# Window attention and experts on one core: the heads of five groups turned on VectorE, shorter weight prefetch, another place for the row scatter

## The chip, the core and the metric

The kernel runs on one core of one Trainium2 chip. The metric is the device time of one execution in microseconds. A core has five engines that run their own instruction streams in order: TensorE (PE in the profile, with its weight loads shown apart as PEld), VectorE (DVE), ScalarE (ACT), GpSimd (POOL) and SyncE (SP, which here only starts transfers). They wait for each other through semaphores.

## What is computed

Two things in a row. First, attention over a window of 64 positions for 8 batches, 8 heads, 576 positions and 64 values a head:

```
scores = (q @ k.T) / 8;  masked where not 0 <= pos_i - pos_j < 64
attn   = exp(scores - max) / (sum + 1e-9)
out    = attn @ v
```

Then each of the 4608 rows (512 values, all heads side by side) goes to one of 8 experts, the one with the largest logit:

```
logits = x @ w_gate + modality_bias[modality_id]
e      = argmax(logits);  gate = softmax(logits)[e]
out    = gate * (relu(x @ w1[e]) @ w2[e])        # w1: 512x1024, w2: 1024x512
```

All in 32-bit floats. The expert matmuls are done with numbers split in two parts (`Whi`, `Wlo` for weights, `xh`, `xl` and `hh`, `hl` for rows), three products for one.

## The kernel before

**Attention** goes in 36 steps `s` of 128 positions (a pair of blocks of 64). Two steps make a group `G`, 18 in all; a group has four blocks. For a step the scores of its blocks need `q` and `k` with the head's values on the partitions, so each group's `q` and `k` are turned first, one step or two ahead: step `s` turns parts of group `s // 2 + 1`, `k` in even steps, `q` in odd ones, four heads in `part(0)` and four in `part(1)`. A part is turned in one of two ways. By TensorE: four 128x128 transposes into a PSUM tile `tp` (`heads_t`, line 594, recorded under the helper's line 470), then a copy out of it on VectorE or ScalarE (`heads_out`, line 605). Or by VectorE alone: one transpose of 32x32 blocks from SBUF to SBUF (`turn_heads`, line 568), which needs the heads loaded in another layout, in pieces of 32 values, by eight requests for four heads (line 590) in place of two (line 584). Before the change seven late groups, those from group 8 on whose four blocks lie in one batch, have four heads in each way.

**Experts** begin while attention is still running: from step 12 on (`FIRST`), each step has up to four gaps, and at each gap `gap(it, True)` records one piece of expert work: six or twelve matmuls of a slot of 256 rows (`first`, line 304, and `second`, line 326). What a piece leaves to other engines is put in `later` and recorded by the next `run_later()`. The end of a slot's first or second 128 rows is `finish` (line 332): VectorE scales the result into a tile `y` (line 334), GpSimd scatters it to the output (line 337).

**Rows** reach the experts through a scratch in HBM: `route1` to `route3` find expert and place, and two scatters by GpSimd (line 809) write a group's rows. From group 4 on they are held back (`held`) and issued by `release()`, which in a step with gaps stands ahead of the first gap. It also records what is left of the routing on VectorE, and the conversion of the indices (line 821).

**Weights** of the first two experts come in 32 raw pieces. Each `weights(s)` call takes one older piece on VectorE (`split_lo`, line 119), one on ScalarE (`split_hi`, line 114), and loads new ones until two are in flight. The raw pieces and the results of `finish` use the same four buffers, `y`. A buffer is given to whoever asks next after its last reader is recorded.

The order on all engines is the order in which this code records instructions (the schedule is manual). `at` is a table of loads by step: values, then `k` or `q` of a later group, all requests on SyncE's queue, recorded at one place in the middle of a step. Group `G >= 8` loads `k` in step `2G-3` and `q` in step `2G-2` into two buffers `qk`; each is turned one step later. The framework gives each request started from SyncE or ScalarE one of eight semaphores in turn, and a request waits until the one that had the semaphore before has landed.

Of the kernel before, what the change touches and what calls it, by code (L numbers as in the profile page):

```python
# [20 lines left out]
W64 = 64  # L21
# [5 lines left out]
def tile_window_attn_moe(  # L27
# [12 lines left out]
    nc = tc.nc  # L40
    B, H, S, D = q.shape
# [4 lines left out]
    HP = H // 2  # L46
    R32 = 32
# [199 lines left out]
    def run_later():  # L247
        while later:
            later.pop(0)()
# [243 lines left out]
    def by_group(x):  # L493
        return x.rearrange("p (a h j) i -> p a h j i", a=2, h=HP)
# [8 lines left out]
    qk = {}  # L503
# [3 lines left out]

    PARTS = ((K0, K1), (Q0, Q1))
    AHEAD = range(1, 8)
    QUARTERS = 8  # L510
    WARM = 8, 3

    n_tp = [0]
# [36 lines left out]
        else:  # L550
            qk[G, nm] = work.tile([P, 2, H, D], F32, name="qk", bufs=2)

    def quartered(G):

        return G >= QUARTERS and GBLK * G // BPB == (GBLK * G + GBLK - 1) // BPB

    def plain(t, nh):

        return t.rearrange("p t h d -> p (t h d)")[:, 0:2 * nh * D].rearrange("p (t h d) -> p t h d", t=2, d=D)

    def by_heads(t):

        return t.rearrange("p t h d -> p (t h d)")[:, H * D:].rearrange("p (h u d) -> p h u d", h=HP // 2, d=R32)

    def turn_heads(G, nm, i):

        dst = by_group(qT if nm == "q" else kT)[:, G % 2, 2 * i:2 * i + 2]
        nc.vector.transpose(
            out=dst.rearrange("p h j i -> p (h j i)"),
            in_=by_heads(qk[G, nm]).rearrange("p h u d -> p (h u d)"))  # L570

    def load_qk(G, nm, blocks=range(GBLK), dma=nc.sync):

        t = qk[G, nm]
        x = q if nm == "q" else k
        i = blocks[0]
        while i <= blocks[-1]:
            b, g = divmod(GBLK * G + i, BPB)
            n = min(BPB - g, blocks[-1] + 1 - i)
            nh = HP if quartered(G) else H  # L580
            src = x[b, 0:nh, g * W64:(g + n) * W64].rearrange("h (p t) d -> p t h d", t=2)
            p0 = i * W64 // 2
            for par in range(2):
                dma.dma_start(out=plain(t, nh)[p0:p0 + n * W64 // 2, par], in_=src[:, par])
            u = slice(i * W64 // R32, (i + n) * W64 // R32)
            for h in range(nh, H):
                for c in range(2):
                    rows = slice((h % 2 * 2 + c) * R32, (h % 2 * 2 + c + 1) * R32)
                    src = x[b, h, g * W64:(g + n) * W64, c * R32:(c + 1) * R32]
                    dma.dma_start(out=by_heads(t)[rows, (h - nh) // 2, u, :],  # L590
                                  in_=src.rearrange("(u p) d -> p u d", p=R32))
            i += n

    def heads_t(G, nm, i, tp):


        src = plain(qk[G, nm], HP if quartered(G) else H).rearrange("p t (h a) d -> p t h (a d)", a=2)
        for h in range(2):
            for t in range(2):
                n = 2 * h + t  # L600
                turn(tp[:, n * P:(n + 1) * P], src[:, t, 2 * i + h])
# [135 lines left out]
    def release():  # L737

        if held:
            tick(len(routing))  # L740
            held.pop(0)()
# [142 lines left out]
    def when(step, f, *args):  # L884
        at.setdefault(max(step, -1), []).append((f, args))
# [9 lines left out]
    for G in range(1, NG):  # L895
        ahead = 1 if G in AHEAD else 0
        for nm, step in (("k", 2 * G - 3 - ahead), ("q", 2 * G - 2 - ahead)):
            when(step, new_qk, G, nm)
            when(step, load_qk, G, nm)

    pieces = []
    raws = []
# [144 lines left out]
    def weights(s):  # L1047

        if halves:
            split_lo(*halves.pop(0))  # L1050
        if len(raws) == 2 or raws and not pieces:
            split_hi(*raws[0])
            halves.append(raws.pop(0))
        while pieces and len(raws) < 2:
            x, c = pieces.pop(0)
            raw = epool.tile([P, WCH], F32, name="y", bufs=4)
            raws.append((load_piece(raw, evs[x], c), x, c))

    for s in range(NPR + 4):
# [7 lines left out]
        heads = PARTS[j] if G < NG else ()  # L1067
        R = (s - 5) // GB if s >= 5 and j == 1 else -1

        def part(i):  # L1070
            if not heads:
                return
            if i == 1 and quartered(G):
                turn_heads(G, *heads[1])
                return
            tp = turn_bank(s)
            heads_t(G, *heads[i], tp)
            heads_out(tp, G, *heads[i], nc.scalar.copy if heads[i] == K1 else nc.vector.tensor_copy)
# [59 lines left out]
            cnt = ranks()  # L1138
            exps(s, (5, 6, 7))
        else:  # L1140
            release()
            gap(it, True)
            run_later()
            tick(2)
            if s < NPR:
                exps(s, (2, 3, 4))
            if s < FIRST + 4 or s % 2:
                weights(s)
            for f, args in at.pop(s, ()):
                f(*args)  # L1150
            gap(it, True)
            cnt = ranks()
            if s < NPR + 2:
# [1 line left out]
            part(0)  # L1155
            run_later()
            tick(n_tick)
            if s < NPR:
                exps(s, (5, 6, 7))
        if n_gap > 2:  # L1160
# [3 lines left out]
        part(1)  # L1164
        run_later()
        tick(n_tick)
        if s == WEIGHTS:
            load_weights()
        if s >= WEIGHTS:
            weights(s)  # L1170
        if n_gap > 3:
            gap(it, True)
        run_later()
# [278 lines left out]
```

## Time and profile before

| | |
|---|---|
| median of 3 runs | 629.34 us (627.99 to 630.23) |
| the profiled execution | 624.07 us, its span 622.3 us |
| granted TensorE clock, mean over the span | 0.989 |
| PE busy | 600.2 us, 96% of the span |
| DVE, ACT, POOL busy | 389.3, 293.7, 140.9 us |

Steps are told apart in the trace by their scores matmuls (line 640), 32 in each step: those of step 16 start at 117.23 us, of step 17 at 127.91, of step 25 at 216.22, of the last, step 35, at 320.84. In the timeline a row has the start, the duration, the engine (PEld and SPq, ACTq are weight loads and transfer starts), the line, the operation, output<-input, the shapes, how many were merged, and in brackets the idle time of the engine ahead of it with what ended it.

### The profile page before, as it was taken

Reading aid. Unit: us, or ns where it says so; the run is one execution under the profiler, and the core shown is the slowest. Engines: PE = TensorE matmul, PEld = TensorE weight load, DVE = VectorE, ACT = ScalarE, POOL = GpSimd, SP = SyncE. Lnnn points to the kernel's source line nnn. Section 1 sums busy time; section 2 is a strip of 40 time slices with the busy share of each in tenths; the row PEclk is TensorE's granted clock in tenths of the full one; section 3 lists DMA queues with packets and bytes.
Section 4 is the critical chain, followed back from the end, with each engine's and each line's share of the span. In section 5 each row is a group of like instructions: output and inputs, shape, how many; then the busy total and the mean of one; then the engine's idle time right before and its main releaser. Section 6 shows DMA issues by size and latency. Waiting matters only on the chain.

```text
span 622.3 us, 17338 instructions
## 1 busy us (share of the span) xinstructions
PE 600.2 (96%) x6309; PEld 537.6 (86%) x6309; DVE 389.3 (63%) x1493; ACT 293.7 (47%) x926; POOL 140.9 (23%) x315
## 2 busy tenths in 40 slices
PE   7999889979999989999999999999999999999996
PEld 5888778868889878988898899899999999989986
DVE  3899988857867776767656365323224734776621
ACT  3899885753756556555553111111112513554411
POOL 6333322132142212320423131011001111102202
PEclk7999999999999999999999999999999999999999
DMA  9998957656757735554513034622243534678300
GB/s 167 219 242 213 223 159 181 158 152 152 171 152 183 197 84 137 154 111 102 148 53 105 35 101 151 188 71 69 44 159 101 171 135 136 190 252 241 114 17 22
DMA packets 175111, 88.08 MB, mean 142 GB/s; under 512 B 138746, under 2 KB 157744, under 8 KB 174896
## 3 DMA queue, kind: packets, MB, share of 16 engines
q1 hardware_dynamic: 166400, 67.46, 44.6%
q0 software_dynamic: 5888, 18.93, 8.1%
q8 instruction: 50, 0.82, 0.5%
q10 hardware_dynamic: 2736, 0.58, 0.5%
q14 instruction: 37, 0.30, 0.2%
HBM read 67.49 MB, written 23.91 MB: 147 GB/s over the span
## 4 chain that ended last, share of the span: by engine, by line
PE 70%; DVE 5%; DMA 5%; SPq 3%; issue 2%; ACT 2%; POOL 1%; POOLq 0%; DVEq 0%; ACTq 0%
PE y L326 27%; PE em L304 19%; PE sp L304 10%; PE tp L470 6%; PE av L696 2%; PE sp L640 2%; DMA out_dram<-y,id 2%; SPq L590 2%; DMA xs_scratch<-xa,idx 1%; PE tp L725 1%; DVE xt L266 1%; PE y L377 1%; DMA xt<-xs_scratch 1%; DVE xl L196 1%; POOL xs_scratch L809 1%
## 5 line engine op out<-in xcount | busy, mean ns | idle before, releaser
L326 PE MATMUL y<-Whi,hh 128*128 128x512 f32 x288 | 116.3, 404 | 0.0
L666 ACT ACTIVATE ss<-ss,mn 128x128 f32<-128x128 f32 x288 | 112.2, 397 | 6.6 <-DVE mn L654 6.6
L326 PE MATMUL y<-Wlo,hh 128*128 128x512 f32 x288 | 113.2, 393 | 0.0
L326 PE MATMUL y<-Whi,hl 128*128 128x512 f32 x288 | 112.9, 392 | 0.0
L313 DVE SCALAR_TENSOR_TENSOR hl<-em,hh 128x512 fp32r<-128x512 f32 x50 | 34.4, 689 | 79.5 <-ACT hh L312 79.1
L337 POOL DMA_INDIRECT out_dram<-y,id x36 | 39.7, 1104 | 191.0 <-DVE y L334 160.8
L304 PE MATMUL em<-xh,Whi 128*128 128x256 f32 x400 | 81.7, 285 | 0.0
L304 PE MATMUL em<-xl,Whi 128*128 128x256 f32 x400 | 79.2, 279 | 0.0
L304 PE MATMUL em<-xh,Wlo 128*128 128x256 f32 x400 | 79.1, 279 | 0.0
L312 ACT ACTIVATE hh<-em 128x512 fp32r<-128x512 f32 x50 | 29.9, 599 | 100.5 <-PE em L304 95.5
L675 ACT COPY pT<-tp 128x512 f32<-128x512 f32 x57 | 31.5, 589 | 83.3 <-PE tp L470 83.0
L809 POOL DMA_INDIRECT xs_scratch<-xa,idx x36 | 36.6, 1017 | 128.9 <-DVE e_n_p L154 58.9
L326 PEld LDWEIGHTS y<-Whi,hl 128*128 128x128 f32 x288 | 54.3, 189 | 12.2
L654 DVE CUSTOM_DVE_ANT_0 ss<-sp,masks 128x128 f32<-128x128 f32 x288 | 63.4, 285 | 2.3 <-PE sp L640 2.3
L304 PEld LDWEIGHTS em<-xh,Whi 128*128 128x128 f32 x400 | 62.8, 188 | 2.3
L326 PEld LDWEIGHTS y<-Whi,hh 128*128 128x128 f32 x288 | 54.7, 190 | 8.9
L326 PEld LDWEIGHTS y<-Wlo,hh 128*128 128x128 f32 x288 | 54.5, 189 | 8.5
L304 PEld LDWEIGHTS em<-xh,Wlo 128*128 128x128 f32 x400 | 60.9, 188 | 0.0
L304 PEld LDWEIGHTS em<-xl,Whi 128*128 128x128 f32 x400 | 60.8, 188 | 0.0
L666 ACT ACTIVATION_READ_ACCUMULATOR ss<-ss,mn 128x1 f32 x288 | 55.9, 194 | 0.0
L312 ACT ACTIVATE hh<-sp 128x512 fp32r<-128x512 f32 x22 | 13.1, 597 | 76.1 <-PE sp L304 76.1
L696 PEld LDWEIGHTS av<-ve,pT 128*64 128x64 f32 x576 | 36.3, 138 | 12.6 <-issue 8.1
(242 smaller groups left out, 1201.7 us busy)
## 6 DMA issues: line engine op xcount, KB each, us to landing
xt<-xs_scratch SPq DMA_DIRECT2D x72, 128.0 KB, 2.9
vo<-in_v_dram SPq DMA_DIRECT2D x32, 256.0 KB, 3.3
y<-in_moe_w_dram SPq DMA_DIRECT2D x32, 256.0 KB, 2.8
vo<-in_moe_w_dram SPq DMA_DIRECT2D x24, 256.0 KB, 3.6
ss<-in_moe_w_dram SPq DMA_DIRECT2D x24, 256.0 KB, 4.2
xs_scratch<-xs_scratch SPq DMA_DIRECT2D x8, 514.0 KB, 5.8
pT<-in_moe_w_dram SPq DMA_DIRECT2D x16, 256.0 KB, 4.5
qk<-in_k_dram SPq DMA_DIRECT2D x22, 128.0 KB, 3.9
```

Of the source, the lines that this page charges most:

```text
L304: nc.tensor.matmul(out=hb[:, i * TP:(i + 1) * TP], lhsT=w[buf][:, c0:c0 + P], rhs=x[:, c * TP:(c + 1) * TP], start=(n == 0), stop=(n == le ...
L312: nc.scalar.activation(out=hh, in_=hb, func=AF.Relu),
L313: nc.vector.scalar_tensor_tensor(out=hl, in0=hb, scalar=0.0, in1=hh.bitcast(F32), op0=ALU.max, op1=ALU.subtract)))
L326: nc.tensor.matmul(out=sl["y", t], lhsT=h[:, i * TP + t * P:i * TP + (t + 1) * P], rhs=w[buf][:, c0:c0 + DM], start=(k == 0 and n == 0), s ...
L337: ins = nc.gpsimd.indirect_dma_start(out=out, out_offset=bass.IndirectOffsetOnAxis(ap=sl["id"][:, t:t + 1], axis=0), in_=y, in_offset=None ...
L470: nc.tensor.transpose(out=out_, in_=in_, identity=ident[p0:p0 + n, p0:p0 + n])
L590: dma.dma_start(out=by_heads(t)[rows, (h - nh) // 2, u, :], in_=src.rearrange("(u p) d -> p u d", p=R32))
L654: nc.vector.tensor_tensor_reduce(out=ss[a][:, hp, :], in0=sp[a][:, hp * P:(hp + 1) * P], in1=mask, scale=-1.0 / 8.0, scalar=3.0e38, op0=AL ...
L666: nc.scalar.activation(out=ss[a][:, hp, :], in_=ss[a][:, hp, :], func=AF.Exp, bias=mn[:, h:h + 1], scale=-1.0, accum_out=sm[:, h:h + 1])
L675: nc.scalar.copy(out=pT, in_=pp)
L696: nc.tensor.matmul(out=by_block(av)[c * W64:(c + 1) * W64, a, :, hp, :], lhsT=pT[:, i:i + W64], rhs=(vo if c else ve)[p][:, 2 * hp + a, :] ...
L809: ins = nc.gpsimd.indirect_dma_start(out=xs, out_offset=bass.IndirectOffsetOnAxis(ap=idx[:, j:j + 1], axis=0), in_=xg[j], in_offset=None)
```

## The change

Four edits.

1. Groups 10, 12, 14, 16 and 17 (`WHOLE`) have all eight heads turned by VectorE. Groups 8 and 9 (`HALF`) stay as they were; the others are turned by TensorE as before. `n_plain(G)` is the number of heads that TensorE turns.
2. In the five groups the loads of all heads are pieces of 32 values: 16 requests for a tensor in place of 10, and every fourth (odd head, second half) is started by ScalarE. From group 8 on a tensor's loads are several entries of the table, for two heads each (the first four heads of a `HALF` group are one entry), and `loads(n)` records them at four places of a step instead of one.
3. From step 16 on, one raw weight piece is in flight instead of two.
4. `release()` stands behind the first gap and `run_later()` instead of ahead of them.

```
-    QUARTERS = 8
+    HALF = 8, 9
+    WHOLE = 10, 12, 14, 16, 17
...
+    def n_plain(G):
+
+        return 0 if G in WHOLE else HP if G in HALF else H
...
     def load_qk(...)
-            for h in range(nh, H):
+            for h in hs if hs[0] >= nh else ():
                 for c in range(2):
...
-                    dma.dma_start(out=by_heads(t)[rows, (h - nh) // 2, u, :],
-                                  in_=src.rearrange("(u p) d -> p u d", p=R32))
+                    other = nh == 0 and h % 2 and c
+                    (nc.scalar if other else dma).dma_start(
+                        out=by_heads(t, nh)[rows, (h - nh) // 2, u, :],
+                        in_=src.rearrange("(u p) d -> p u d", p=R32))
...
-            when(step, load_qk, G, nm)
+            for h in (0, *range(max(n_plain(G), 2), H, 2)) if n_plain(G) < H else (0,):
+                when(step, load_qk, G, nm, range(GBLK), nc.sync, range(h, h + 2))
...
     def weights(s):
-        if len(raws) == 2 or raws and not pieces:
+        n = 2 if s < FIRST + 4 else 1
+        if len(raws) >= n or raws and not pieces:
...
-        while pieces and len(raws) < 2:
+        while pieces and len(raws) < n:
...
         def part(i):
-            if i == 1 and quartered(G):
-                turn_heads(G, *heads[1])
+            if 2 * 2 * i >= n_plain(G):
+                turn_heads(G, *heads[i])
                 return
...
         else:
-            release()
             gap(it, True)
             run_later()
+            release()
             tick(2)
...
-            for f, args in at.pop(s, ()):
-                f(*args)
+            loads(3)
...
             run_later()
             tick(n_tick)
+            loads(1)
...
         part(1)
         run_later()
         tick(n_tick)
+        if s > FIRST:
+            loads(1)
...
         if s >= WEIGHTS:
             weights(s)
+        if s > FIRST:
+            loads(9)
```

How the order of instructions moves, at three places. First GpSimd at step 16, which is the first of six steps (16, 20, 24, 28, 32, 36) in which a held pair of row scatters meets the result of a slot (`xs_scratch<-xa` is the scatter of rows, `out_dram<-y` that of a result). Before:

```order
L808 COPY xa_101<-idc 128x1
L809 DMA xs_scratch<-xa_101,idx 39168x514
L808 COPY xa_102<-idc 128x1
L809 DMA xs_scratch<-xa_102,idx 39168x514
L336 MEMSET pause 1x1
L337 DMA out_dram<-y,id 4608x512
```

and now:

```order
L336 MEMSET pause 1x1
L337 DMA out_dram<-y,id 4608x512
L814 COPY xa_101<-idc 128x1
L815 DMA xs_scratch<-xa_101,idx 39168x514
L814 COPY xa_102<-idc 128x1
L815 DMA xs_scratch<-xa_102,idx 39168x514
```

The result's scatter has moved ahead of the two row scatters; the same holds on VectorE, where line 334 moves ahead of the six routing instructions and of the index conversion. The second result of the same slot keeps its place, four instructions behind the last of these. In the change it has the buffer of the first result in steps 16, 20 and 24; before it had it in 16 and 24.

Second, TensorE in step 18, from the turning of attention's output (`xa`) to the next expert matmul. Before:

```order
L470 MATMUL tp<-ident_r,xa_102 128x128 x4
L470 MATMUL tp<-ident_r,qk 128x128 x4
L326 MATMUL y_2908<-Whi_65,hh 128x512
```

and now:

```order
L470 MATMUL tp<-ident_r,xa_102 128x128 x4
L326 MATMUL y_2904<-Whi_65,hh 128x512
```

Four transposes are gone; the same happens in ten steps (17 is still a `HALF` step; 18, 19, 22, 23, 26, 27, 30, 31, 32, 33 are the ten). On VectorE one `COPY kT<-tp` or `qT<-tp` becomes a `STREAM_TRANSPOSE kT<-qk` or `qT<-qk` at the same place in each of them.

Third, ScalarE in step 18, where `q` of group 10 is loaded. Before:

```order
L666 ACTIVATE ss,sm<-ss,mn 128x128 x3
L717 COPY xaT<-tp 128x512
L312 ACTIVATE hh<-em 128x512
L666 ACTIVATE ss,sm<-ss,mn 128x128 x3
L114 CAST Whi_2524<-y 128x512
L675 COPY pT<-tp 128x512 x2
```

and now:

```order
L672 ACTIVATE ss,sm<-ss,mn 128x128 x3
L595 DMA qk<-in_q_dram 32x8x32
L723 COPY xaT<-tp 128x512
L312 ACTIVATE hh<-em 128x512
L595 DMA qk<-in_q_dram 32x8x32
L672 ACTIVATE ss,sm<-ss,mn 128x128 x3
L595 DMA qk<-in_q_dram 32x8x32
L114 CAST Whi_2520<-y 128x512
L595 DMA qk<-in_q_dram 32x8x32
L681 COPY pT<-tp 128x512 x2
```

Four transfer starts now stand between the exponentials and copies of a step; ScalarE gets 40 of them in all, in steps 17, 18, 21, 22, 25, 26, 29, 30, 31 and 32.

More of the change, by code (lines that the diff above doesn't have):

```diff
@@ L551, in new_qk, with by_heads, load_qk @@
             qk[G, nm] = work.tile([P, 2, H, D], F32, name="qk", bufs=2)
-    def quartered(G):
-        return G >= QUARTERS and GBLK * G // BPB == (GBLK * G + GBLK - 1) // BPB
+    def n_plain(G):
+        return 0 if G in WHOLE else HP if G in HALF else H
     def plain(t, nh):
         return t.rearrange("p t h d -> p (t h d)")[:, 0:2 * nh * D].rearrange("p (t h d) -> p t h d", t=2, d=D)
-    def by_heads(t):
-        return t.rearrange("p t h d -> p (t h d)")[:, H * D:].rearrange("p (h u d) -> p h u d", h=HP // 2, d=R32)
+    def by_heads(t, nh):
+        x = t.rearrange("p t h d -> p (t h d)")[:, 2 * nh * D:]
+        return x.rearrange("p (h u d) -> p h u d", h=(H - nh) // 2, d=R32)
     def turn_heads(G, nm, i):
         dst = by_group(qT if nm == "q" else kT)[:, G % 2, 2 * i:2 * i + 2]
+        src = by_heads(qk[G, nm], n_plain(G))
+        n = 2 * i - n_plain(G) // 2
         nc.vector.transpose(
             out=dst.rearrange("p h j i -> p (h j i)"),
-            in_=by_heads(qk[G, nm]).rearrange("p h u d -> p (h u d)"))
-    def load_qk(G, nm, blocks=range(GBLK), dma=nc.sync):
+            in_=src[:, n:n + 2].rearrange("p h u d -> p (h u d)"))
+    def load_qk(G, nm, blocks=range(GBLK), dma=nc.sync, hs=range(H)):
         t = qk[G, nm]
         x = q if nm == "q" else k
+        nh = n_plain(G)
         i = blocks[0]
@@ L579, in load_qk @@
             n = min(BPB - g, blocks[-1] + 1 - i)
-            nh = HP if quartered(G) else H
-            src = x[b, 0:nh, g * W64:(g + n) * W64].rearrange("h (p t) d -> p t h d", t=2)
             p0 = i * W64 // 2
-            for par in range(2):
+            for par in range(2 if hs[0] < nh else 0):
+                src = x[b, 0:nh, g * W64:(g + n) * W64].rearrange("h (p t) d -> p t h d", t=2)
                 dma.dma_start(out=plain(t, nh)[p0:p0 + n * W64 // 2, par], in_=src[:, par])
             u = slice(i * W64 // R32, (i + n) * W64 // R32)
-            for h in range(nh, H):
+            for h in hs if hs[0] >= nh else ():
                 for c in range(2):
@@ L589, in load_qk @@
                     src = x[b, h, g * W64:(g + n) * W64, c * R32:(c + 1) * R32]
-                    dma.dma_start(out=by_heads(t)[rows, (h - nh) // 2, u, :],
-                                  in_=src.rearrange("(u p) d -> p u d", p=R32))
+                    other = nh == 0 and h % 2 and c
+                    (nc.scalar if other else dma).dma_start(
+                        out=by_heads(t, nh)[rows, (h - nh) // 2, u, :],
+                        in_=src.rearrange("(u p) d -> p u d", p=R32))
             i += n
     def heads_t(G, nm, i, tp):
-        src = plain(qk[G, nm], HP if quartered(G) else H).rearrange("p t (h a) d -> p t h (a d)", a=2)
+        src = plain(qk[G, nm], n_plain(G)).rearrange("p t (h a) d -> p t h (a d)", a=2)
         for h in range(2):
@@ L1068, in tile_window_attn_moe, with loads @@
         R = (s - 5) // GB if s >= 5 and j == 1 else -1
+        def loads(n):
+            for f, args in at.get(s, [])[:n]:
+                f(*args)
+            at[s] = at.get(s, [])[n:]
         def part(i):
```

## The prediction

> **What bounds the kernel now.** I read the page first, then busy time by stretches, then the waits inside the stretches that were too long.
>
> ```profile
> PE 600.2 (96%) x6309; PEld 537.6 (86%) x6309; DVE 389.3 (63%) x1493; ACT 293.7 (47%) x926; POOL 140.9 (23%) x315
> PE 70%; DVE 5%; DMA 5%; SPq 3%; issue 2%; ACT 2%; POOL 1%; POOLq 0%; DVEq 0%; ACTq 0%
> ```
>
> TensorE is busy 96% of the span and holds 70% of the chain of waits. An average hides stages, so here are five steps and the long stretch behind step 17 (length, busy time of PE, PEld, DVE, ACT, POOL, granted clock, DMA share, GB/s): step 16, then 17, 21, 25 and 29, which come at the same place of their four-step round, then all from step 18 on up to the last 11 us.
>
> ```profile
> 117.23:127.91 10.68, 10.24 (x138) 9.02 (x136) 9.28 (x36) 5.95 (x22) 4.29 (x8) 1.00 0.67 163
> 127.91:143.92 16.01, 12.30 (x142) 10.44 (x140) 7.73 (x34) 6.35 (x22) 3.74 (x8) 0.89 0.53 134
> 174.79:185.48 10.69, 10.69 (x146) 9.52 (x144) 7.70 (x34) 6.24 (x22) 3.20 (x6) 1.00 0.62 166
> 216.22:229.14 12.92, 10.99 (x145) 9.50 (x143) 7.80 (x34) 5.85 (x21) 2.88 (x6) 1.00 0.48 120
> 259.95:270.74 10.79, 10.79 (x145) 9.52 (x143) 6.05 (x31) 5.23 (x20) 2.87 (x6) 1.00 0.58 139
> 143.92:611.00 467.08, 464.67 (x4285) 418.88 (x4284) 272.26 (x928) 187.80 (x537) 88.51 (x184) 1.00 0.47 130
> ```
>
> Steps 21 and 29 are all TensorE. Step 17 has 3.71 us without it and a clock of 0.89, step 25 has 1.93 us without it. From step 18 on to 611 us it is idle for 467.08 - 464.67 = 2.4 us, step 25's 1.93 among them, so time that TensorE saves in this stage reaches the end. Why steps 17 and 25 are long the timeline of VectorE, GpSimd and TensorE says:
>
> ```profile
> 121.86 0.43 DVE L543 COPY ve<-vo 64x512 f32<-64x512 f32 x1
> 123.51 0.75 DVE L334 TENSOR_SCALAR y<-y,gate 128x512 f32<-128x512 f32 x1
> 124.39 1.05 POOL L809 DMA_INDIRECT xs_scratch<-xa,idx  x1 [5.74 <-DVE y L334]
> 125.92 0.96 POOL L809 DMA_INDIRECT xs_scratch<-xa,idx  x1 [0.28 <-POOL xa L808]
> 126.86 0.68 DVE L119 TENSOR_TENSOR Wlo<-y,Whi 128x512 fp32r<-128x512 f32 x1
> 127.19 1.22 POOL L337 DMA_INDIRECT out_dram<-y,id  x1 [0.22 <-DVE hl L313]
> 132.68 0.75 DVE L334 TENSOR_SCALAR y<-y,gate 128x512 f32<-128x512 f32 x1 [5.14 <-DMA out_dram<-y,id]
> 133.71 0.99 POOL L337 DMA_INDIRECT out_dram<-y,id  x1 [5.25 <-DVE rw L704]
> 137.24 0.15 DVE L790 TENSOR_TENSOR tgt<-tp,ebase 128x16 f32<-128x16 f32 x1
> 137.50 1.08 PE L470 MATMUL tp<-ident_r,qk 128*128 128x128 f32 x4 [2.40 <-issue]
> 215.05 1.00 POOL L337 DMA_INDIRECT out_dram<-y,id  x1 [0.22 <-issue]
> 218.94 0.75 DVE L334 TENSOR_SCALAR y<-y,gate 128x512 f32<-128x512 f32 x1 [2.99 <-DMA out_dram<-y,id]
> PE tp L470 <- DVE lg L730: 1.9, 1, 1.9
> ```
>
> A slot's second result is written into the buffer of its first. So VectorE stands still for 5.14 us until the first one's scatter has landed, and that scatter sits on GpSimd behind two row scatters. TensorE then finds its PSUM tile unread (line 790 empties it at 137.24, the transposes start at 137.50). The same in step 25 with 2.99 us; its row of the waits is the last above.
>
> **Part by part. The transposes.**
>
> ```profile
> 295.84 0.60 PE L470 MATMUL tp<-ident_r,xa 128*128 128x128 f32 x4
> 296.27 0.60 PE L470 MATMUL tp<-ident_r,qk 128*128 128x128 f32 x4
> 296.63 0.37 PE L304 MATMUL em<-xh,Whi 128*128 128x256 f32 x1
> L605 DVE COPY kT<-tp x13: 673/691/694, 33.8 to 296.9; 128x512 f32<-128x512 f32 x13
> L568 DVE STREAM_TRANSPOSE qT<-qk x7: 704/711/714, 116.7 to 309.2; 128x512 f32<-128x512 f32 x7
> ```
>
> A set of four costs TensorE what it shifts the next start: 296.27 - 295.84 = 0.43 us (durations overlap, starts don't). Ten sets are 4.3 us, on the path in full, since in these steps TensorE is busy all the time. VectorE swaps a copy of 691 ns for a transpose of 711 ns: ten times 0.02 us, nothing, and it waits for TensorE no more.
>
> **The scatter and the weights.** With line 334 right behind the copy of line 543 it ends at 122.29 + 0.75 = 123.04. From result to scatter took 0.28 us (133.43 to 133.71), so the scatter starts at 123.32.
>
> ```profile
> L337 POOL DMA_INDIRECT out_dram<-y,id x36: 966/994/1778, 127.2 to 612.0; - x36
> DMA to landing us min/median/max: 2.7/4.1/6.8
>   DVE y L334: 8.1, 2
> ```
>
> It lands 2.7, 4.1 or at most 6.8 us later: at 126.0, 127.4 or 130.1. The second result is due at 126.86 + 0.68 = 127.54, so VectorE's wait of 5.14 us becomes 0, 0 or 2.6 us. How much of such a wait reaches TensorE: 5.14 cost 3.71, 2.99 cost 1.93, so about 1.1 us are covered. I take the median landing, for the scatter is now first in its queue: no loss. Steps 17 and 25 then take the 10.74 us of 21 and 29 (mean): 5.27 + 2.18 = 7.4 us. The last row shows these two waits as the only ones of this kind. Because one buffer now serves both results in steps 16, 20 and 24, the bad end is three waits of 2.6 us, 1.5 us of each uncovered: 4.5 us to take off. The row scatters come later by one scatter, about 1 us (994 ns), and one line 334; GpSimd, busy 23%, has room. With one piece ahead a raw weight has half a step, some 5 us, to land. It needs 2.8 us:
>
> ```profile
> y<-in_moe_w_dram SPq DMA_DIRECT2D x32, 256.0 KB, 2.8
> ```
>
> Of the 7.4 us, 1.6 are TensorE at half clock (12.30 us busy in step 17 for work that takes 10.69). The Trainium skill, "TensorE: Matmul & The Clock Gate", section "What's actually happening", gives an idle window of about 3.4 us for the drop to half. Here the longest pause was 2.40 us, with two shorter ones ahead of it, so the trace does not fit a single such window. Taken strictly, that rule would leave the half clock in place; that is a rival below.
>
> **The requests.**
>
> ```profile
> L590 SPq DMA_DIRECT2D qk<-in_k_dram x56: 448/451/1959, 89.2 to 285.8; - x56
> L584 ACTq DMA_DIRECT2D qk<-in_q_dram x4: 648/657/722, 0.8 to 2.9; - x4
>   PE tp L470: 66.6, 20
> 292.87 1.07 ACT L675 COPY pT<-tp 128x512 f32<-128x512 f32 x2 [2.27 <-PE tp L470]
> qk<-in_q_dram SPq DMA_DIRECT2D x56, 32.0 KB, 2.3
> q1 hardware_dynamic: 166400, 67.46, 44.6%
> 196.80 2.44 SPq L211 DMA_DIRECT2D xt<-xs_scratch  x5
> xt<-xs_scratch SPq DMA_DIRECT2D x72, 128.0 KB, 2.9
> 202.81 0.70 DVE L266 STREAM_TRANSPOSE xt<-xt 128x512 f32<-128x512 f32 x1
> ```
>
> ScalarE started no transfer in this stage before, so its four per step are bounded: 4 x 0.451 = 1.8 us by SyncE's median for this shape, or three at its own 0.722 and one at SyncE's longest, 1.959: 4.1 us. Queued behind them are the exponentials, the copies `xaT` and `pT`, `hh` and `split_hi`, for which TensorE and VectorE wait. ScalarE idles before a step's first `pT` copy, waiting for TensorE: 66.6 us in 20 steps from 127 to 322 us, 3.3 us each, 2.27 us at the least (behind step 31); and the ten steps get 0.43 us shorter. At 1.8 us a step all is covered; at 4.1 us 4.1 - (3.3 - 0.4) = 1.2 us a step stay uncovered, 12 us in ten. A request also waits for the eighth before it to land; ScalarE's stand every fourth, so mostly for its own older ones or for SyncE's of microseconds ago (2.3 us to land). The shape is SyncE's, so I go by its median, near the low end, and take 1 us lost in all for a long start or two.
>
> SyncE has two starts more per tensor (12 against 10): about 1 us a step. The rows of the next slot, started at 196.80, are with VectorE at 196.80 + 2.44 + 2.9 = 202.1, and it takes them at 202.81. If SyncE is late by 2 us there (two tensors ahead of it), VectorE loses 1.3 us, of which its 1.1 us of cover leave little. I take 0.3 us; bounds 0 and 1.3. The requests are needed a whole step later, 10 us, so their own landing is hidden unless it triples.
>
> Runs of 256 bytes become twice as many of 128: 1024 packets more per tensor. At the mean of 44.6% x 16 x 622.3 / 166400 = 27 ns these cost 1.7 us a step on 16 engines, which are busy 53 to 67% in the steps above: room enough. The skill's "DMA: Bandwidth & Descriptors", "Specifications", gives 512 bytes as the least size for full rate, which speaks against the edit; the trace shows 32 KB in 128-byte runs landing in 2.3 us all the same, and by either the loads stay hidden.
>
> **Sum.** 4.3 + 7.4 - 1.0 - 0.3 = 10.4 us off the profiled 624.07 (span 622.3 and 1.8 around it): 613.7. The runs shown have a median of 629.34, 5.3 us above that execution, for a reason the profile doesn't show; I take the same difference off it: **619.0 us**, 1.6% faster.
>
> **Rivals.**
>
> *The half clock stays* (0.07): the drop at 137.5 does not come from the pause ahead of it. For: the 1.93 us without TensorE in step 25 left the clock at 1.00. Against: from step 18 on to 611 us, with shorter pauses alone, the clock is 1.00. 1.6 us less gain: 620.6.
>
> *The transposes come back as waits* (0.15): VectorE, busy 9.28 of 10.68 us in step 16, sets the pace of the ten steps, and TensorE's 4.3 us turn into waits for it. For: line 790 and 730 hold PSUM. Against: TensorE is at 100% in steps 21 and 29, with VectorE at 7.7 and 6.1. 623.3.
>
> *The shared buffer still stalls* (0.15): the result's scatter lands after 5.5 to 6.8 us as the one at 127.19 did (to 132.68), now in three steps, and the half clock with it. 4.5 + 1.6 us less: 625.1.
>
> *ScalarE's queue is held* (0.11), the slower side: a start on ScalarE does not return before earlier transfers drain, as SyncE's longest of 1.96 us show. Four such in a step are 7.8 us, less some 3.3 us of idle time: 4.5 us in each of ten steps, 45 us at the extreme. The gain is used up at 11.7 / 10 + 3.3 = 4.5 us a step, 1.1 us per request. At 1.3 us it is 629.34 - 11.4 + 10 x (5.2 - 3.3) = 637. Against: SyncE's median of 0.45 us.
>
> *The change doesn't do what it says* (0.04): the loads on two queues wait for each other's semaphores so that transposes on VectorE come late; near 629.
>
> **Chances.** The forecast has 0.48. By 0.3% (1.9 us, what a measurement can tell here from nothing): forecast, clock, transposes and buffer cases are faster, at most 0.01 of them not: 0.84; within: 0.07; slower: 0.09. The likeliest case alone spans 616.5 (no loss by requests, and 1 us of small waits before transposes gone) to 621.5 (a late landing in one step, 3 us held on ScalarE). The range takes in the transposes and buffer cases, **615.5 to 626**.
>
> **What would show it.** Right: step 17 and step 25 near 10.7 us with no row of VectorE's line 334 waiting for `out_dram`; steps 18, 19, 22, 23, 26, 27 and 30 to 33 shorter by 0.43 us; clock 1.00 in step 17; ScalarE's starts near 0.5 us. Wrong: line 334 waiting in steps 17, 21 or 25; idle time of TensorE before `tp<-ss` released by ScalarE; starts on ScalarE's queue above 1.1 us; VectorE's line 266 or 568 waiting for a DMA.

## The result, and the profile after

The change takes 619.57 us (median of 4 runs, 617.16 to 620.38) beside 628.66 us for the kernel before: a ratio of 0.985, 95% interval 0.981 to 0.989. Measured once more later, it came to 0.990 (0.986 to 0.993). The profiled execution took 617.16 us, span 615.3 us, 6.9 us less than the profiled one of before. The forecast of 619.0 us holds. Its parts do not all hold, and that is what the experiments are about.

From the page of the change, busy times and the chain of waits:

```profile
PE 592.0 (96%) x6269; PEld 528.9 (86%) x6269; DVE 389.3 (63%) x1493; ACT 293.0 (48%) x926; POOL 140.3 (23%) x315
PE 75%; DVE 6%; ACT 2%; DMA 2%; issue 2%; SPq 1%; POOL 0%; POOLq 0%; DVEq 0%; ACTq 0%
```

TensorE is busy for 8.2 us less. Of these 5.2 lie in steps 16 to 34 (40 matmuls fewer, and no half clock in step 17) and 3.1 ahead of step 16, where the kernel before ran 10.2 us at half clock in this profile and the change none. And 2% of the chain has gone from SyncE's queue and 3% from DMAs to TensorE. Now steps 16, 17, 20, 21, 24, 25 and 33, and the long stretch from step 18 to 604 us, as busy time by stretches (length, then PE, PEld, DVE, ACT, POOL, granted clock, DMA share, GB/s):

```profile
115.70:126.78 11.08, 10.47 (x136) 9.15 (x132) 9.39 (x37) 6.07 (x23) 4.39 (x9) 1.00 0.76 184
126.78:138.49 11.71, 10.42 (x139) 9.10 (x136) 7.81 (x34) 6.35 (x22) 2.86 (x6) 1.00 0.60 130
157.73:170.65 12.92, 11.14 (x140) 9.46 (x137) 10.13 (x43) 8.05 (x26) 4.75 (x9) 1.00 0.75 207
170.65:181.38 10.73, 10.73 (x145) 9.55 (x141) 7.69 (x34) 6.15 (x22) 2.86 (x6) 1.00 0.69 151
200.65:212.05 11.40, 10.90 (x140) 9.48 (x136) 9.32 (x44) 6.57 (x24) 4.31 (x8) 1.00 0.86 232
212.05:222.79 10.74, 10.74 (x144) 9.56 (x140) 7.73 (x35) 5.63 (x21) 2.87 (x6) 1.00 0.39 77
293.13:303.87 10.74, 9.91 (x135) 8.66 (x132) 6.06 (x31) 5.33 (x20) 2.86 (x6) 1.00 0.71 166
138.49:604.00 465.51, 461.27 (x4247) 415.03 (x4244) 272.20 (x928) 187.56 (x537) 89.35 (x184) 1.00 0.48 131
```

Step 17 fell from 16.01 to 11.71 us, its clock is 1.00 again, and step 25 is all TensorE. But in the long stretch TensorE now stands for 4.2 us where it stood for 2.4: step 20 is 2.2 us longer than before, 24 is 0.9 longer, and steps 16, 32 and 33 0.3 to 0.6. From the first score of step 16 to that of step 35 the time went from 203.61 to 197.73 us, 5.9 us less; 1.5 us more were gained ahead of step 16, and 0.4 us lost behind step 35. Ahead of step 16 the change moves only two starts of raw weights on SyncE's queue (in steps 13 and 14). Step 16 starts at 115.7 to 118.3 us in the fourteen profiles of this study, in the two of the change at 115.70 and at 118.32. So the 1.5 us aren't put down to the change, and kernels are compared below by their steps 16 to 34, and by ratios.

The stall that edit 4 was to remove, in the timelines of VectorE, GpSimd and ScalarE of the change:

```profile
120.81 0.75 DVE L334 TENSOR_SCALAR y<-y,gate 128x512 f32<-128x512 f32 x1
121.85 1.05 POOL L337 DMA_INDIRECT out_dram<-y,id  x1 [5.10 <-DVE lg L759]
121.89 0.22 ACT L762 ACTIVATE ex<-lg 128x16 f32<-128x16 f32 x1 [2.00 <-DVE lg L759]
123.66 0.98 POOL L815 DMA_INDIRECT xs_scratch<-xa,idx  x1 [0.55 <-DVE kT L611]
126.61 0.75 DVE L334 TENSOR_SCALAR y<-y,gate 128x512 f32<-128x512 f32 x1
```

and, from the view of line 334 over the whole span, all that VectorE sat idle for ahead of it (us, times):

```profile
  PE y L326: 11.1, 8
```

The first result's scatter starts at 121.85, ahead of the rows' scatters, and the second result (126.61) waits for nothing; `out_dram` is gone from line 334's waits. The third row of the timeline shows something the prediction had not counted: the routing now stands behind line 334 on VectorE, so ScalarE stands for 2.00 us at the routing's exponential (1.34 us at the same place before), with the next exponentials queued behind it.

Step 20's new loss. First SyncE's request for the next slot's rows in the kernel before (five transfers together), for comparison:

```profile
155.06 3.04 SPq L211 DMA_DIRECT2D xt<-xs_scratch  x5
```

Then the timelines of SyncE, VectorE and TensorE of the change:

```profile
151.95 0.33 SPq L211 DMA_DIRECT2D xt<-xs_scratch  x1
156.60 1.30 DVE L266 STREAM_TRANSPOSE xt<-xt 128x512 f32<-128x512 f32 x2 [1.18 <-DMA xt<-xs_scratch]
158.34 0.69 DVE L572 STREAM_TRANSPOSE qT<-qk 128x512 f32<-128x512 f32 x1
159.09 0.67 PE L646 MATMUL sp<-kT,qT 64*64 64x128 f32 x16 [0.69 <-DVE qT L572]
161.01 0.15 DVE L736 TENSOR_TENSOR lg<-tp,bias_sel 128x8 f32<-128x8 f32 x1
161.22 0.66 PE L470 MATMUL tp<-ident_r,ss 128*128 128x128 f32 x4 [0.88 <-DVE lg L736]
```

and a row of its waits from 155 to 175 us (us in total, times, longest):

```profile
ACT Whi L114 <- DMA y<-in_moe_w_dram: 1.8, 1, 1.8
```

The next slot's rows are asked for at 151.95, 3.92 us into step 19; before it was 1.14 us into it (155.06, step 19 starting at 153.92). VectorE waits 1.18 us for them; the transpose of `qT` comes behind that, and TensorE waits 0.69 us for it; the logits' sum (line 736) comes behind the rows' split, and TensorE waits another 0.88 us. The raw weights stand behind the rows on SyncE's queue, so ScalarE waits 1.8 us for them too; no wait of TensorE in this step is put down to that. Slow transfers weren't the reason: the piece asked for at 154.68 is with ScalarE at 157.68, 3.0 us later, beside the usual 2.8. The requests came late, not the landings.

### The profile page after: what moved, and what is told of

Same layout as the page of the kernel before. It is cut to its first block, busy times and chain, and to the rows that moved or that the text cites. A ratio compares the mean times of both kernels' runs of the same rounds, so it can differ in the third digit from the quotient of the medians.

```text
span 615.3 us, 17370 instructions
## 1 busy us (share of the span) xinstructions
PE 592.0 (96%) x6269; PEld 528.9 (86%) x6269; DVE 389.3 (63%) x1493; ACT 293.0 (48%) x926; POOL 140.3 (23%) x315
## 4 chain that ended last, share of the span: by engine, by line
PE 75%; DVE 6%; ACT 2%; DMA 2%; issue 2%; SPq 1%; POOL 0%; POOLq 0%; DVEq 0%; ACTq 0%
PE y L326 29%; PE em L304 20%; PE sp L304 10%; PE tp L470 6%; PE av L702 3%; PE sp L646 3%; PE tp L731 1%; DVE ss L660 1%; DMA xt<-xs_scratch 1%; PE y L377 1%; ACT ss L672 1%; DVE xl L196 1%; DMA xs_scratch<-xa,idx 1%; DVE xa L713 1%; DVE xt L266 1%
## 5 line engine op out<-in xcount | busy, mean ns | idle before, releaser
L326 PE MATMUL y<-Whi,hh 128*128 128x512 f32 x288 | 115.7, 402 | 0.0
```

What stands on the lines that cost most here:

```text
L326: nc.tensor.matmul(out=sl["y", t], lhsT=h[:, i * TP + t * P:i * TP + (t + 1) * P], rhs=w[buf][:, c0:c0 + DM], start=(k == 0 and n == 0), s ...
```

## The experiments

The twelve kernels ran in three sets of four, each set beside its own runs of the kernel before (medians 626.70, 625.12 and 625.79 us). Lengths of steps, in us, from the starts of the scores, each from one profile:

| kernel | ratio (95%) | step 16 | 17 | 20 | 24 | 25 | 33 | steps 16 to 34 |
|---|---|---|---|---|---|---|---|---|
| before | 1 | 10.68 | 16.01 | 10.75 | 10.52 | 12.93 | 10.15 | 203.6 |
| the change | 0.985 (0.981, 0.989) | 11.08 | 11.71 | 12.92 | 11.40 | 10.74 | 10.74 | 197.7 |
| `release_only` | 0.987 (0.984, 0.990) | 11.03 | 11.17 | 11.04 | 10.92 | 10.73 | 10.15 | 197.7 |
| `ahead_only` | 1.000 (0.999, 1.002) | 11.56 | 11.50 | 10.89 | 11.17 | 12.43 | 11.22 | 204.6 |
| `turns_only` | 1.004 (1.002, 1.006) | 11.02 | 13.42 | 15.07 | 12.88 | 12.16 | 15.25 | 210.3 |
| `ex_behind` | 0.992 (0.990, 0.995) | 10.95 | 11.34 | 14.50 | 11.55 | 11.40 | 11.37 | 200.5 |
| `all_sync` | 0.988 (0.986, 0.991) | 11.02 | 11.67 | 11.46 | 11.62 | 10.73 | 10.77 | 197.6 |
| `one_place` | 0.985 (0.983, 0.987) | 11.20 | 11.66 | 12.85 | 11.40 | 10.72 | 9.69 | 196.5 |
| `no_ahead` | 0.991 (0.989, 0.993) | 11.01 | 11.15 | 14.57 | 14.20 | 10.74 | 10.90 | 201.5 |
| `rows_first` | 1.002 (1.001, 1.004) | 11.20 | 11.18 | 14.93 | 16.42 | 10.73 | 10.83 | 205.4 |
| `change_again` | 0.990 (0.986, 0.993) | 11.05 | 11.76 | 14.16 | 11.83 | 10.72 | 10.79 | 199.6 |
| `two_groups` | 0.987 (0.984, 0.991) | 11.10 | 11.70 | 11.02 | 11.35 | 10.74 | 10.12 | 197.1 |
| `two_groups_ex` | 0.986 (0.983, 0.989) | 11.02 | 11.37 | 10.58 | 10.66 | 10.71 | 11.25 | 196.9 |
| `sync_one_ex` | 0.993 (0.991, 0.995) | 11.03 | 10.22 | 16.21 | 11.33 | 10.74 | 14.54 | 203.3 |

Some of these lengths have half clock in them, which the last section shows to hang partly on chance: step 17 of the kernel before, step 20 of `turns_only`, `ex_behind`, `no_ahead`, `rows_first`, `change_again` and `sync_one_ex`, step 24 of `no_ahead` and `rows_first`, step 33 of `turns_only` and `sync_one_ex`.

**Edit 4 alone** (`release_only`), on the kernel before:

```diff
-            release()
             gap(it, True)
             run_later()
+            release()
             tick(2)
```

> The kernel before with edit 4 alone (a group's row scatters behind the copy, the result and its scatter). The prediction's working: the waits of line 334 in steps 17 and 25 go, 7.4 us, so about 621.3 against a kernel before of 628.7; step 17 near 10.7 us. Rival, from the trace of the change: the routing now stands behind line 334 on VectorE, so ScalarE stands 2.0 us at the routing's exponential in steps 16, 20, 24, 28 and 32 and part of it reaches TensorE; 1 us or so in each of three steps makes it about 624.5, with steps 16, 20 or 24 longer than before.

618.09 us. Steps 16, 17, 20 and 24 of this kernel, as busy time by stretches:

```profile
117.50:128.52 11.02, 10.47 (x135) 9.14 (x132) 9.31 (x36) 5.94 (x22) 4.39 (x9) 1.00 0.72 180
128.52:139.69 11.17, 10.44 (x140) 9.10 (x137) 8.01 (x34) 6.35 (x22) 3.18 (x6) 1.00 0.62 160
159.76:170.80 11.04, 10.83 (x141) 9.48 (x137) 8.17 (x34) 6.37 (x23) 3.95 (x8) 1.00 0.70 183
201.84:212.76 10.92, 10.70 (x141) 9.48 (x137) 8.92 (x43) 6.34 (x23) 3.50 (x6) 1.00 0.75 192
```

This one line has the whole gain: its ratio of 0.987 lies between the change's two, and its steps 16 to 34 take as long as the change's, 197.7 us. Steps 17 and 25 give back 4.84 + 2.20 = 7.0 us, close to the 7.4 of the prediction. The rival was right as well, with less: steps 16, 20 and 24 are 0.35, 0.29 and 0.40 us longer than before, 1.0 us in all. ScalarE's stand at the routing's exponential is 2.00, 2.00 and 1.93 us there, for 1.34, 1.34 and 1.28 before; that this is what they pay for is argued, and the pair `two_groups` and `two_groups_ex` below bears it out in steps 20 and 24.

**Edit 3 alone** (`ahead_only`), on the kernel before:

```diff
-        if len(raws) == 2 or raws and not pieces:
+        n = 2 if s < FIRST + 4 else 1
+        if len(raws) >= n or raws and not pieces:
...
-        while pieces and len(raws) < 2:
+        while pieces and len(raws) < n:
```

> The kernel before with edit 3 alone (one raw piece ahead from step 16). The prediction's working: a group's two results then share a buffer in each of three rounds while the first scatter still starts late, so line 334 waits for out_dram in steps 17, 21 and 25: 2 to 4 us on top, 631 to 633. Rival: fewer raw pieces leave a buffer free and the waits go by this edit alone: about 621.

625.87 us beside 626.70: no difference, and neither theory. What VectorE's line 334 waits for here (us, times):

```profile
  DMA out_dram<-y,id: 5.9, 2
```

and steps 17, 21 and 25 by stretches:

```profile
128.80:140.31 11.51, 10.96 (x137) 9.37 (x136) 7.24 (x33) 6.25 (x22) 2.84 (x6) 1.00 0.63 147
171.27:183.80 12.53, 11.05 (x140) 9.54 (x139) 7.81 (x34) 6.35 (x22) 2.88 (x6) 1.00 0.78 191
215.20:227.63 12.43, 11.01 (x141) 9.51 (x141) 7.82 (x34) 5.85 (x21) 2.89 (x6) 1.00 0.46 111
```

The stall leaves step 17, where it also brought the half clock, and appears in step 21, which was clean. So edit 3 does share the buffer of both results in the later rounds, as the prediction said, but it does not add three stalls to two; it moves one. The 4.5 us won in step 17 are lost again: 1.8 in step 21, and 0.6 to 1.1 in each of steps 16, 24, 29 and 33, for which no run here shows the reason.

**Edits 1 and 2 alone** (`turns_only`): the change with both of the diffs above taken back.

> The change without edits 3 and 4, so the transposes on VectorE and the requests alone. The prediction's working: 4.3 us less on TensorE and 1.3 us lost to requests: 625.7 against 628.7, the waits of line 334 in steps 17 and 25 and the half clock kept. Rival, that SyncE's requests come so late that the next slot's rows reach VectorE after TensorE wants them in steps 19 and 20: 2 us more lost there, so 627.5, with step 20 longer than before. Rival, that the whole gain of the change is the transposes: 619.6.

628.83 us, 0.4% slower than before (interval 0.2% to 0.6%): worse than all three expectations. Steps 17, 20 and 33:

```profile
127.33:140.74 13.41, 10.90 (x138) 9.26 (x136) 7.73 (x34) 6.46 (x22) 2.84 (x7) 1.00 0.52 124
159.97:175.05 15.08, 12.50 (x141) 10.72 (x137) 11.16 (x44) 7.82 (x25) 5.36 (x11) 0.89 0.69 179
301.78:317.03 15.25, 13.76 (x133) 11.54 (x132) 5.99 (x30) 5.33 (x20) 3.01 (x8) 0.78 0.56 133
```

The transposes do save what was forecast: steps 18, 19, 22, 23, 26, 27, 30 and 31 are each 0.4 to 0.6 us shorter than before. More than that is lost in steps 20, 24 and 33, and the clock column shows half clock in 20 and 33, where the kernel before had none. The second theory, SyncE's late requests, had the place right and was too small: the rows are asked for 5.0 us into step 19 (1.1 before), VectorE waits 2.13 us for them, and TensorE 2.0 us for the `qT` behind them.

**The release behind three exponentials** (`ex_behind`), on the change; `sync_one_ex` and `two_groups_ex` have it too:

```diff
             gap(it, True)
             run_later()
-            release()
-            tick(2)
             if s < NPR:
                 exps(s, (2, 3, 4))
+            release()
+            tick(2)
```

> The change with the release moved once more, behind the exponentials of three units (VectorE's order stays, on ScalarE the routing's exponential comes after three others). If ScalarE's stand of 2.0 us at the routing's exponential is what makes steps 16, 17, 20 and 24 longer than their neighbours in the change: 2 to 3.5 us less, 616 to 617.5, and VectorE's wait of 1.4 us before line 313 in step 16 goes. If those steps are long for the late rows and weights alone: 619.6, no change.

621.53 us, a miss. ScalarE's stand at the routing's exponential fell from 2.00 to 0.84 us, and steps 16 and 17 got 0.13 and 0.37 us shorter; but steps 20 (14.50, at a clock of 0.88), 25 and 33 got longer. Step 20 has its rows asked for 4.6 us into step 19, still later than in the change; the order on ScalarE was not what made it long. In step 25 line 334 waits for a scatter again, 1.37 us.

**All requests on SyncE** (`all_sync`), on the change:

```diff
-                    other = nh == 0 and h % 2 and c
+                    other = False
```

> The change with every request on SyncE's queue, none on ScalarE's. Theory A, SyncE is held by ScalarE's requests: each of those stands in ScalarE's program order, and SyncE's next ones wait for it (in the change SyncE starts nothing between 5.4 and 9.1 us of step 17, while ScalarE's come at 7.2, 8.0 and 8.4). Then that hole of 3.7 us goes, four starts of 0.48 us a step come in, the next slot's rows are asked for before 3 us of step 19 and step 20 falls from 12.9 to about 11.1: 617.5. Theory B, SyncE is late by the number of its starts: 8 more in two steps are 3.9 us, the rows are asked for after 5 us of step 19, step 20 takes 13 us or more: 621 to 625.

618.30 us. First the hole: ScalarE's and SyncE's requests of step 17 (it starts at 126.78) in the change, then SyncE's in `all_sync` (step 17 starts at 128.22), both by timeline:

```profile
131.93 0.31 SPq L595 DMA_DIRECT2D qk<-in_k_dram  x1
133.97 0.32 ACTq L595 DMA_DIRECT2D qk<-in_k_dram  x1
134.77 0.32 ACTq L595 DMA_DIRECT2D qk<-in_k_dram  x1
135.16 0.44 ACTq L595 DMA_DIRECT2D qk<-in_k_dram  x1
135.86 0.31 SPq L595 DMA_DIRECT2D qk<-in_k_dram  x1
```

```profile
129.29 7.43 SPq L595 DMA_DIRECT2D qk<-in_k_dram  x12
```

a row of SyncE's own waits in the change from 120 to 150 us (us in total, times, longest):

```profile
SPq L595 <- DMA qk<-in_k_dram: 3.6, 1, 3.6
```

and step 20 of `all_sync` by stretches:

```profile
160.06:171.53 11.47, 10.92 (x141) 9.48 (x137) 8.67 (x36) 6.54 (x24) 3.49 (x6) 1.00 0.59 170
```

In the change SyncE starts nothing from 132.24 to 135.86. Its next request uses the same semaphore as ScalarE's of 133.97 and waits until that one has landed (at 135.84), and ScalarE had started it only when its program order came to it. Alone on the queue SyncE starts twelve without a break. The rows are asked for 1.6 us into step 19, and step 20 falls from 12.92 to 11.47: theory A at this place. Yet the sum of the steps is the change's (197.6 against 197.7), because step 19 takes 10.63 us for 9.69. So the hole is a cause of step 20's loss, and taking it away by putting all starts on SyncE wins nothing.

**Requests in one place** (`one_place`), on the change:

```diff
-            loads(3)
+            loads(99)
```

> The change with all requests of a step in one place, as before (VectorE's transposes and the two queues stay). Theory A (SyncE held by ScalarE's late requests): ScalarE's four stand early in the step behind three exponentials, SyncE's hole in step 17 shrinks, the rows are asked for before 3 us of step 19, step 20 falls to about 11.2: 617.5. If it is the number of starts (theory B): the same lateness, 619.6.

616.23 us, ratio 0.985 (0.983 to 0.987). ScalarE's four of step 17 now come between 4.3 and 6.2 us of the step and SyncE's hole is 1.8 us, but the rows are asked for 3.6 us into step 19 and step 20 stays at 12.85: theory A's expectation for that step fell. What it wins is step 33, 9.69 for 10.74.

**Two raw pieces ahead** (`no_ahead`): the change with edit 3's diff taken back.

> The change without edit 3 (two raw pieces ahead throughout). If the single raw piece makes ScalarE wait for its weights in step 20 (1.84 us at line 114 in the change): that wait goes and 0.5 to 1 us with it, 618.7 to 619. If edit 3 is needed for the second results' buffer: line 334 waits for out_dram in step 17 or 25 again, 621 or more. If neither: 619.6.

620.05 us. No row of line 334 waits for `out_dram`: with edit 4 in, edit 3 is not needed for that. But steps 20 and 24 take 14.57 and 14.20 us, each with a stretch at half clock. The rows are asked for later (4.6 and 4.1 us into steps 19 and 23, for 3.9 and 2.5), because a raw piece that gets its buffer only 5.7 us into step 17 stands ahead of that step's requests on SyncE's queue: these start at 6.7 us, for 1.1 in the change. None of the three expectations said that.

**The rows one place earlier** (`rows_first`), on the change:

```diff
-                    if k == 2 and t == 1 and nxt is None:
+                    if k == 2 and t == 0 and nxt is None:
```

> The change with the next slot's rows asked for one place earlier, ahead of the last requests of a q tensor on SyncE's queue. If the rows' late request (3.9 us into step 19) makes step 20 long: it comes 1.5 to 2.5 us earlier, VectorE's line 266 no longer waits for xt, and step 20 falls from 12.9 to about 11.1: 617.5. If step 20 is long because the DMA engines themselves are full there (share 0.9 to 1.17 from 156 to 163 us) or by ScalarE's wait for its weights: little changes, 619 to 619.6.

626.38 us, 0.2% slower than the kernel before. SyncE's queue from step 19 on (it starts at 148.54), by timeline:

```profile
149.85 2.73 SPq L211 DMA_DIRECT2D xt<-xs_scratch  x5
152.62 1.45 SPq L595 DMA_DIRECT2D qk<-in_q_dram  x3
154.32 0.37 SPq L103 DMA_DIRECT2D y<-in_moe_w_dram  x1
```

and rows of its waits from 158 to 175 us (us in total, times, longest):

```profile
DVE hl L313 <- ACT hh L312: 6.3, 2, 4.0
PE sp L646 <- DVE qT L572: 2.5, 1, 2.5
```

The rows did come 2.6 us earlier (1.3 us into the step), and VectorE waits for them no more. But the raw weight that was asked for 0.4 us into step 19 in the change now comes at 5.8 us. ScalarE waits for it with `hh` queued behind, VectorE waits 4.0 us for `hh`, the last transpose of `qT` comes behind that, and TensorE stands for 2.5 us. Rows, weights and requests stand in one queue, and what is put ahead in it makes the rest late.

**The change once more** (`change_again`), and **all heads on VectorE in groups 14 and 16 only** (`two_groups`; groups 10, 12 and 17 half and half as before):

```diff
-    HALF = 8, 9
-    WHOLE = 10, 12, 14, 16, 17
+    HALF = 8, 9, 10, 12, 17
+    WHOLE = 14, 16
```

> The change once more, beside the next three on the same chip. If steps 17, 20, 24, 32 and 33 are long by the order of the work: the same steps are long again, 16 to 35 take 197.7 us, 617 to 620 and a ratio to before near 0.986. If step 20's 12.9 us were chance: it is shorter here.

> The change with all heads turned by VectorE in two of the five groups only (14 and 16); groups 10, 12 and 17 stay half and half, as before. If the loss in steps 20, 24 and 33 comes from the requests of 10, 12 and 17, which SyncE starts right ahead of a slot's rows and weights: those steps fall to those of the kernel with edit 4 alone (11.04, 10.92, 10.15), steps 26, 27, 30 and 31 stay at 9.56 to 9.71, and steps 16 to 35 take 195.6 to 196.2 us against 197.7: 2 us less than the change. If the loss comes from one raw piece ahead or from the release: steps 20 and 24 stay at 12.9 and 11.4, and 1.7 us are lost by the six transposes given up: about 1.7 us more than the change.

619.11 and 618.19 us. The same steps of the change are long again; step 20 is even longer, 14.16, with half clock in it. `two_groups`, steps 20, 24 and 33:

```profile
160.23:171.25 11.02, 10.81 (x140) 9.48 (x136) 8.22 (x35) 6.36 (x23) 3.51 (x6) 1.00 0.61 178
202.28:213.63 11.35, 10.91 (x141) 9.47 (x137) 9.28 (x43) 6.45 (x23) 4.94 (x9) 1.00 0.83 221
294.79:304.91 10.12, 10.12 (x137) 9.10 (x136) 6.03 (x30) 5.23 (x20) 2.87 (x6) 1.00 0.48 125
```

Steps 20 and 33 fall to those of edit 4 alone (11.04 and 10.15), and steps 26, 27, 30 and 31 keep their 9.56 to 9.71. So the loss of step 20 belongs to group 10's requests, and that of step 33, in this pair of runs, to group 17's (`two_groups_ex`, which hasn't these either, has 11.25 there, so they can't be the whole of it). Groups 10 and 12 save 1.8 us in steps 18, 19, 22 and 23 and lose 1.9 in step 20 alone. Step 24 stays at 11.35: its loss isn't group 12's. The sum is 0.6 us less than in the change's first profile (2.4 less than in `change_again`, whose step 20 has half clock in it), not the 1.5 to 2.1 expected: step 17 stays at 11.70 where edit 4 alone has 11.17. That half microsecond is in every kernel with edits 3 and 4 in which ScalarE's exponentials stand behind the release, and in neither that has edit 4 without edit 3 (`release_only`, `no_ahead`); `rows_first` (11.18) is an exception without an explanation.

**Two combinations.**

> As the one before, and the release behind three exponentials. ScalarE's stand of 2.0 us at the routing's exponential falls to about 0.8; the steps 16, 20 and 24, which edit 4 alone made 0.3 to 0.4 us longer, give that back: 1 us less than the one before. If the earlier run's loss in step 20 with this order (14.5 us) belongs to the order itself: step 20 is over 13 us here too, and it is slower than the one before.

> The change with every request on SyncE's queue and in one place, and the release behind three exponentials. SyncE's hole in step 17 and the late requests at a step's end both go: rows asked for before 2 us of step 19, step 20 at 11.1 to 11.5, step 24 near 11, steps 16 to 35 in 195.5 to 196.5 us, 2 us less than the change. If the number of starts on SyncE is what costs: rows asked for after 3 us of step 19 and no gain on the change.

617.32 and 621.55 us. In `two_groups_ex` steps 20 and 24 take 10.58 and 10.66, 0.4 and 0.7 us less than with the release's order of the change; steps 29 and 33 take most of it back (11.40 and 11.25 for 10.83 and 10.12). Where rows and weights are in time, the order on ScalarE is worth something; behind late rows it isn't seen. `sync_one_ex` has its rows asked for 4.6 us into step 19 and its step 20 at 16.21, with 6.8 us at half clock in it: what theory B said. But `all_sync`, with the same 16 starts of SyncE for a tensor, has its rows asked for 1.6 us into step 19. The number of starts alone doesn't settle it; what separates the two kernels (one place for the requests, the release further back) wasn't taken apart.

No kernel here is shown to beat the change: the lowest, `one_place` (0.985) and `two_groups_ex` (0.986), have intervals that overlap with its own.

## Why the prediction was right

The number came out within 0.6 us, and that is partly luck. The mechanism that carries the result, the stall in steps 17 and 25, was right and nearly of the size forecast. The transposes' gain was right too, but the loss by late rows, put at 0.3 us, and smaller losses used it up.

*Steps 17 and 25, 7.4 us.* Right in mechanism, and the only part that carries the result. The change gives 4.30 + 2.19 = 6.5 us, edit 4 alone 7.0. No wait of line 334 for a scatter is left, the scatter landed in time with both results in one buffer, and step 17's clock is 1.00: the rivals of the shared buffer and of the half clock in step 17 fell for the change. The margin is thin: waits of line 334 for a scatter are back in `ex_behind` (1.37 us, step 25) and `sync_one_ex` (0.95 us). Missing was the release's own price: with the routing behind line 334, steps 16, 20 and 24 are 0.3 to 0.4 us longer each.

*Transposes, 4.3 us in ten steps.* Eight of them gave 4.0 us, 0.50 each for 0.43. Steps 32 and 33 came out 0.9 us longer instead.

*Requests on ScalarE, 1.0 us.* The price of a start was right, and better than taken: 0.318 us at the median, the longest 1.80, and only two of 40 take over 0.5 us. In `all_sync`, where ScalarE has none, steps 18, 22, 26 and 30 take the same 9.5 to 9.6 us, so the starts cost TensorE nothing that these steps show. The rival of a held ScalarE queue fell. Failed has the sentence that a request waits "mostly for its own older ones or for SyncE's of microseconds ago": SyncE waits for ScalarE's, 3.6 us in step 17. Rows of the change's line 595 (minimum, median, longest in ns):

```profile
L595 ACTq DMA_DIRECT2D qk<-in_k_dram x20: 317/318/1802, 131.2 to 279.8; - x20
L595 SPq DMA_DIRECT2D qk<-in_k_dram x76: 311/449/2093, 87.8 to 287.0; - x76
```

*SyncE's later rows, 0.3 us, bounds 0 and 1.3.* This step failed. The prediction named the place and foresaw 2 us of lateness (it was 2.8) and 1.3 us of waiting on VectorE (1.18), but took VectorE's cover of 1.1 us, measured at another wait, as good here. Step 20 lost 2.2 us, 1.9 more than with groups 14 and 16 alone, for a reason it left out: a `qT` transpose that TensorE needs at once, and then the logits' sum, stand behind those rows on VectorE (0.69 and 0.88 us of waiting on TensorE). One of the prediction's own signs of being wrong, line 266 waiting for a DMA, is what the trace of the change shows.

*The sum.* 10.4 us forecast; from step 16 to 35 the profile shows 4.0 + 6.5 - 4.6 = 5.9, the 4.6 being what the other steps got longer, nearly all of it in steps 16, 20, 24, 28, 32 and 33. The other 1.5 us of that profile lie ahead of step 16, where two executions of the change itself differ by 2.6. By medians the gain was 9.1 us in the first measurement and 6.7 in the last. That the first came so near to the forecast is luck: its parts as measured add up to 5.9.

*The rival of transposes that come back as waits* (0.15) is the one nearest to the truth for edits 1 and 2, with another engine: not VectorE's pace, but SyncE's queue ahead of VectorE gives their 4 us back.

Still open: which of edit 3 and the spread requests makes step 24 half a microsecond longer than with edit 4 alone, why step 19 of `all_sync` takes 0.9 us more, and what makes step 33 long where the rows aren't late.

## What to carry to other kernels

When a change has several parts, run each alone: here one moved line was worth all of the gain, and 40 matmuls less on the engine with 96% of the span were worth nothing that could be measured, since the loads that they needed came ahead of other loads in a full queue. Of requests that are added to a queue, ask what is asked for next on it, who takes that first, and what stands behind it there. Requests of one stream that are dealt out to two engines can tie the two together: here they take their semaphores from one set, and SyncE's next request waited until ScalarE had come to its own.

## What was not expected of the hardware

**Half clock after short pauses, and by the luck of a grid.** In each of the fourteen traces the granted clock changes only at points that are whole multiples of 3.413 us apart (in `change_again` half clock begins at 82.05 and 163.97 us, 24 x 3.413 us between them). So the stretches of this grid are what to look at. First two with half clock right behind them, in step 17 of the kernel before and in step 20 of `change_again`, and the stretch at half clock that follows in `change_again`; then two that kept full clock, in step 20 of the change's first profile and in step 25 of the kernel before; last the one ahead of the half clock in step 33 of `sync_one_ex`. The busy time of TensorE is the second number, the granted clock the third from the end:

```profile
134.05:137.46 3.41, 0.66 (x4) 0.42 (x4) 3.28 (x21) 2.77 (x12) 1.50 (x3) 1.00 0.20 77
160.56:163.97 3.41, 1.73 (x36) 1.08 (x31) 3.41 (x12) 2.20 (x4) 1.78 (x3) 1.00 0.91 226
163.98:167.39 3.41, 3.41 (x10) 2.90 (x11) 2.90 (x19) 1.36 (x5) 0.00 (x0) 0.50 0.78 178
157.65:161.06 3.41, 2.00 (x42) 1.32 (x38) 3.41 (x12) 2.24 (x4) 1.26 (x3) 1.00 1.00 243
215.97:219.38 3.41, 1.92 (x47) 1.48 (x44) 0.44 (x1) 0.59 (x1) 0.13 (x2) 1.00 0.83 220
295.60:299.01 3.41, 2.54 (x59) 1.97 (x57) 1.56 (x3) 0.00 (x0) 2.67 (x5) 1.00 0.81 220
```

Half clock begins eleven times between steps 16 and 35 in the fourteen profiles. Ahead of nine of these TensorE was busy for 0.66 to 1.73 us of the grid's stretch, and no stretch of steps 16 to 34 with so little kept full clock: the emptiest that did has 1.83 us (`turns_only`, 133.91:137.32). The other two, with half clock in step 33 (2.20 us in `turns_only`, 2.54 in `sync_one_ex`), don't fit, so busy time isn't all that decides. Step 20 has two pauses of TensorE in both profiles of the change. In `change_again` both (0.67 and 1.02 us) fall into one stretch; in the first profile a border of the grid, at 161.06, cuts the second (0.69 and 0.88 us), and the clock stays. Step 20 takes 14.16 and 12.92 us. So a late load can cost 1.2 us more or not, by where the grid happens to lie, and the change sits at that edge.

The half clock lasts one such stretch or two in these steps (3.41 or 6.83 us). The Trainium skill, "TensorE: Matmul & The Clock Gate", section "What's actually happening", has an idle window of about 3.4 us ahead of it; here what stood ahead was a stretch of that length with much less work, not one of no work.

**The start of a transfer takes longer right behind another.** The rows of line 595 above look as if a start were cheaper on ScalarE's queue than on SyncE's for the same shape, 0.318 us against 0.449 at the median. It is the spacing. In the change, starts that come 0.2 us or more after the end of the one before take 0.318 us on ScalarE (median of 30) and 0.312 on SyncE (17); those within 0.1 us of it take 0.461 (9) and 0.451 (128). The two timelines of step 17 above show both: 0.31 to 0.32 us after a pause on either queue, 0.44 us for ScalarE's of 135.16, right behind another.
